# Sums of weights moved from GpSimd to VectorE, a new place for second-layer blocks, and one rectification in place of two

## The chip, the cores and the metric

The kernel runs on one core of a Trainium2 chip. The metric is the device time of one execution in microseconds. TensorE (PE in the profile) multiplies, VectorE (DVE), ScalarE (ACT) and GpSimd (POOL) work on elements, and SyncE (SP) issues the transfers. Each engine takes its instructions in order.

## The reference

Three stages follow each other; the change lies in the third, a mixture of four experts over all 2304 tokens.

```
attention through 32 memory slots     -> x: 2304 tokens x 512
x = relu(x @ w_in)**2 @ w_out         # 512 -> 2048 -> 512
p = domain_probs / sum(domain_probs)
for e in range(4):                    # moe2_w1: 512 -> 1024, moe2_w2: 1024 -> 512
    h = max(x @ w1[e], 0)
    out += p[:, e:e+1] * (h @ w2[e])
```

## The kernel before

Every float32 operand of a product is held as two parts, a high one and the low remainder. A product takes three matmuls for each piece of the contraction: high by high, high by low, low by high. The helper that makes the parts (`into`, lines 243 to 246, and `rectified`, lines 500 to 505) is a ScalarE instruction for the high part and a VectorE instruction for the low part.

The third stage goes over the 16 slabs `s` of 256 hidden units (four for each expert) twice. The first pass takes tokens 0 to 1023, the second tokens 1024 to 2047 and the last 256 tokens, called the rest.

**First pass.** The first layer of a slab is a 2 by 2 block product with seven products in place of eight, named b11, t1, b21, t2, t3, t4 and b22 in this order (`first_products`, line 507). Each product is two pieces of the contraction by three matmuls, six matmuls of 128x512. They add up in four PSUM banks u, m, v and t: u collects b11, then t2, then t3, and ScalarE copies it out (`copied`, line 526, copies `cc` or a copy that seeds another bank) after each, before the next product may add to it. v is seeded from u after b11, t from u after t3. `total` (line 561) completes one of four hidden blocks g11, g22, g21, g12: an addition on VectorE where a copy of u belongs to it (line 565), and then `rectified`. m holds t1 and b22; the addition for g22 reads m before b22 may add to it, and the addition for g12 empties m for the next slab.

The second layer of a slab is eight plain blocks (`second_l2`, line 476) of six matmuls each, for 128 tokens; the first four read g11 and g21, the last four g12 and g22. They use four PSUM banks in turn, and VectorE takes each into the accumulator (`taken`, line 493; ScalarE does it for the first slab). They are put into the list `todo` and issued during the first layer of the next slab, by `between` (line 820).

The weights of the pass come from the generator `weights` (line 253). For a slab it loads `ra`, the first layer's four blocks, splits two of them, forms four 128x256 sums (`combined`, line 301, into the tiles `s`) and splits these; then it does the same with `rb`, the second layer's. The sums are needed by the first layer's products (from `ra`) and, for the second pass, by its second layer (from `rb`). All parts are also written to DRAM for the second pass (`keep`). Four steps of the generator come after each slab in the source. The tiles `s` have one buffer each, `raw` has two, the first layer's weights have eight and the second layer's four.

**Second pass.** Both layers use seven products (`third_blocks`, line 586, `third_product`, line 624), in an order written out in `STEPS` and `LAST` (lines 619 and 620). The first slab's products run with the last eight blocks of the first pass between them (line 837). For the rest, `rest_l1` (line 667) multiplies the two halves f of a slab's hidden units, 12 matmuls of 128x256 each, into two banks of one PSUM tile, and rectifies each half by itself. `rest_l2` (line 680) of the slab before follows it. The PSUM tiles `two` have two buffers.

The order of the source is a priority, not the order on the engines: a planner at build time orders each engine's instructions by its own estimate of when their inputs are there, so a later instruction can be placed ahead of an earlier one.

Of the kernel before, what the change touches and what calls it, by code (L numbers as in the profile page):

```python
# [12 lines left out]
F32 = mybir.dt.float32  # L13
F32R = mybir.dt.float32r
AF = mybir.ActivationFunctionType
ALU = mybir.AluOpType
# [6 lines left out]
KT = DM // 128  # L23
# [5 lines left out]
NF2 = FS2 // 128  # L29
SE = F2 // FS2  # L30
S2 = E * SE
NB = 512
# [3 lines left out]
NR = NT - 4 * NB  # L36
# [3 lines left out]
def tile_kernel(  # L40
# [11 lines left out]
    nc = tc.nc  # L52
# [12 lines left out]
    def bank(tag):  # L65
        return (ps if tag in ("moe", "score") else ps_one).tile([128, 512], F32, tag=tag, name=tag, bufs=BANKS[tag])
# [234 lines left out]
    def combined(a11, a12, a21, a22, places):  # L301

        u = [p.tile([128, WC], F32, tag=tag, name=f"s{i}", bufs=1) for i, (p, tag) in enumerate(places)]
        t = [u[i // 2][:, (i % 2) * 256:(i % 2 + 1) * 256] for i in range(4)]
        nc.gpsimd.tensor_tensor(out=t[0], in0=a21, in1=a22, op=ALU.add)
        nc.gpsimd.tensor_tensor(out=t[1], in0=t[0], in1=a11, op=ALU.subtract)
        nc.gpsimd.tensor_tensor(out=t[2], in0=a11, in1=a21, op=ALU.subtract)
        nc.gpsimd.tensor_tensor(out=t[3], in0=a12, in1=t[1], op=ALU.subtract)
        return u

    kept = {}
# [150 lines left out]
    def rest():  # L462
        v = halves(8, KT, NR)
        for k in range(KT):
            put((v[:, 0, k], v[:, 1, k]), yacc[:, k, 4 * NB:])
        return v
# [33 lines left out]
    def rectified(c, n, g):  # L500
        nc.scalar.activation(g[:, 0, :n], c, AF.Relu)
        nc.vector.scalar_tensor_tensor(  # L502
            out=g[:, 1, :n], in0=c, scalar=0.0, in1=g[:, 0, :n].bitcast(F32), op0=ALU.max, op1=ALU.subtract
        )
        return g

    def first_products(w, x, total, seeded):

        def block(t, c):
            return [[w[t][:, h, c * 256 + k * 128:c * 256 + (k + 1) * 128] for k in range(2)] for h in range(2)]  # L510

        a = {"b11": (0, 0), "b21": (0, 1), "t1": (2, 0), "t4": (1, 1), "t2": (2, 1), "t3": (3, 0), "b22": (3, 1)}

        def product(po, name, first=True):
            wb, xb = block(*a[name]), x[name]
            i = 0
            for k in range(2):
                for lw, rx in ((0, 0), (0, 1), (1, 0)):
                    nc.tensor.matmul(  # L519
                        po, wb[lw][k], xb[:, rx, k], start=(first and i == 0), stop=(i == 5),  # L520
                        skip_group_check=not first,
                    )
                    i += 1

        def copied(p, seed=None):
            if seed is not None and seeded:
                nc.scalar.copy(seed, p)
                return None
            c = cp[0].tile([128, NB], F32, tag="c", name="cc")
            nc.scalar.copy(c, p)  # L530
            return c

        u, m, v, t = bank("moe"), bank("moe"), bank("moe"), bank("score")
        product(u, "b11")
        u1 = copied(u, v)
        yield
        product(m, "t1")
        yield
        product(v, "b21", first=not seeded)
        total("11", v, u1)  # L540
        yield
        product(u, "t2", first=False)
        u2 = copied(u)
        yield
        product(u, "t3", first=False)
        u3 = copied(u)
        total("22", m, u3)
        if seeded:
            copied(u, t)
        yield  # L550
        product(t, "t4", first=not seeded)
        total("21", t, None if seeded else u3)
        yield
        product(m, "b22", first=False)
        total("12", m, u2)
        yield

    def second_pair(s, x, between):
        g = {}

        def total(name, p, q):
            c = p
            if q is not None:
                c = cp[0].tile([128, NB], F32, tag="c", name="c")
                nc.vector.tensor_tensor(out=c, in0=p, in1=q, op=ALU.add)
            g[name] = rectified(c, NB, hp3[0].tile([128, 2, NB], F32R, tag="g", name="g"))

        for i, _ in enumerate(first_products(w_two[0, s], x, total, s > 0)):
            if i in (4, 5):
                between(i - 4)  # L570
        return [
            (lambda q=q: second_l2(s, q, (g["11"], g["21"]) if q < 4 else (g["12"], g["22"]), (q % 4) * 128))
            for q in range(8)
        ]
# [4 lines left out]
    def shares_of(e):  # L579
        nc.sync.dma_start(out=shares, in_=kept_p[e].partition_broadcast(128).rearrange("p (k n) -> p k n", k=KT))  # L580
# [83 lines left out]
            nc.vector.tensor_tensor(out=m[:, a], in0=po[:, a], in1=m[:, a], op=ALU.add)  # L664
            nc.sync.dma_start(out=outT[o:o + 128, j * NB:(j + 1) * NB], in_=m[:, a])

    def rest_l1(s, x, f, g, two):
        w = w_two[1, s]
        ph = two[:, f]
        i = 0  # L670
        for k in range(KT):
            for lw, rx in ((0, 0), (0, 1), (1, 0)):
                nc.tensor.matmul(  # L673
                    ph[:, :NR], w[f][:, lw, k * 128:(k + 1) * 128], x[:, rx, k],
                    start=(i == 0), stop=(i == 3 * KT - 1),
                )
                i += 1
        rectified(ph[:, :NR], NR, g[:, f])

    def rest_l2(s, g, ps_two):  # L680
        e = s // SE
# [43 lines left out]
    with tc.tile_pool(name="bdp", bufs=1) as bdp, tc.tile_pool(name="cv", bufs=1) as cv, \  # L725
# [6 lines left out]
        with tc.tile_pool(name="att", bufs=2) as att, tc.tile_pool(name="hp1", bufs=2) as hp, \  # L732
# [13 lines left out]
            for t in FIRST_LOADS.split():  # L746
                i = int(t[1])
# [8 lines left out]
            for t in PROGRAM.split():  # L756
                i = int(t[1]) if len(t) > 1 else 0
# [17 lines left out]
            out=p_sb, in0=p_sb, in1=p_sum.unsqueeze(2).to_broadcast([128, NT // 128, E]), op=ALU.mult  # L775
# [13 lines left out]
        with tc.tile_pool(name="ring", bufs=1) as rp, tc.tile_pool(name="tmp3", bufs=2) as tmp:  # L789
            ring = [rp.tile([128, KT, RING], F32R, name=f"ring{i}") for i in range(2)]  # L790
            for s in range(2, N1):
                last = s + 1 == N1
                for j in range(2 * B):
# [8 lines left out]
                    if last and j >= 4:  # L802
                        for _ in range(1 if j == 7 else 2):
                            x = next(steps)
            flush()
    with tc.tile_pool(name="cp2", bufs=6) as cp2, tc.tile_pool(name="w2p", bufs=4) as w2, \
            tc.tile_pool(name="hp3", bufs=6) as hp:
        cp.append(cp2)
        w2p.append(w2)
        hp3.append(hp)  # L810
        next(ws)
        next(ws)
        for e in range(E):
            nc.sync.dma_start(out=kept_p[e].rearrange("(t p) -> p t", p=128), in_=p_sb[:, 8:16, e])
        xr = rest()
        shares_of(0)
        later = []
        todo = []

        def between(i):  # L820
            for _ in range((len(todo) + 1) // 2 if i == 0 else len(todo)):
                todo.pop(0)()

        for s in range(S2):
            todo += second_pair(s, x, between)
            if s + 1 < S2:
                for _ in range(4):
                    next(ws)
        fetch(0)
        for x in prepare(1):  # L830
            pass

        def rest_tile():
            return hp.tile([128, 2, 2, NR], F32R, tag="g", name="gr")

        blocks, g = third_blocks(0, x, later)
        for i, _ in enumerate(blocks):
            if i in (4, 5):
                between(i - 4)
        singles.close()  # L840
        gr = rest_tile()
        later.pop(0)()
        with tc.tile_pool(name="ps_two", bufs=2, space=bass.MemoryType.PSUM) as ps_two:
            two = ps_two.tile([128, 2, NB], F32, tag="two", name="two")
            rest_l1(0, xr, 0, gr, two)
            rest_l1(0, xr, 1, gr, two)
            for s in range(1, S2):
                fetch(s)
                if s % SE == 0:
                    shares_of(s // SE)  # L850
                blocks, g_next = third_blocks(s, x, later)
                gr_next = rest_tile()
                for step in STEPS if s + 1 < S2 else LAST:
                    if step == "p":
                        next(blocks)
                    elif step == "t":
                        later.pop(0)()
                    elif step in A2:
                        third_product(s - 1, g, step, ps_two)
                    elif step[0] == "r":  # L860
                        two = ps_two.tile([128, 2, NB], F32, tag="two", name="two")
                        for f in range(NF2):
                            rest_l1(s, xr, f, gr_next, two)
                    elif step == "e":
                        rest_l2(s - 1, gr, ps_two)
                    else:
                        gather(step[:2], step[3:5], nc.gpsimd if step.endswith("*") else None)
                g, gr = g_next, gr_next
            rest_l2(S2 - 1, gr, ps_two)
            for i, j in ((0, 0), (1, 0), (0, 1), (1, 1)):  # L870
                third_plain(g, i, j, ps_two)
# [52 lines left out]
```

## Time and profile before

| | |
|---|---|
| median of three runs | 1144.48 us (1142.22 to 1147.76) |
| profiled execution | 1143.0 us, of which the span is 1141.2 us |
| busy, share of the span | TensorE 97%, VectorE 73%, ScalarE 52%, GpSimd 12% |
| granted TensorE clock, mean | 0.99 |
| first pass on TensorE | 399 us to 746 us of the span |

Times in the profile are microseconds from the start of the span. The busy share of TensorE counts matmuls that overlap in its pipeline, so it is no measure of lost time by itself; the distance between the starts of successive groups of matmuls is used for that. "Idle before" in square brackets is the time for which the engine did nothing before the instruction, with the instruction that released it.

### The profile page before, as it was taken

What the parts mean: (1) busy time and instruction counts of PE and PEld (TensorE: products, weight loads), DVE (VectorE), ACT (ScalarE), POOL (GpSimd) and SP (SyncE); (2) the same over time, 40 slices, a digit from 0 to 9 for tenths busy, and PEclk for the clock granted to TensorE, in tenths of its full rate; (3) what the DMA queues carried; (4) which work ended last, traced back from release to release, by engine and by line L of the source; (5) the groups of instructions that cost most, each with busy time, mean ns of one, the idle gap of its engine ahead of it and who ended that gap; (6) DMA issues with size and microseconds to landing.
All of it is one profiled execution on the core that took longest, in us unless ns stands there. A gap on an engine that the chain in (4) does not pass through costs nothing.

```text
span 1141.2 us, 16527 instructions
## 1 busy us (share of the span) xinstructions
PE 1101.7 (97%) x6142; PEld 934.8 (82%) x6142; DVE 827.4 (73%) x1366; ACT 589.0 (52%) x1178; POOL 132.3 (12%) x150
## 2 busy tenths in 40 slices
PE   5888999999999999999999999999999999999997
PEld 2667898999999977787888888888888888888886
DVE  6997989786446667768676776866766677776676
ACT  3776666565456464444444444355555555545541
POOL 0032000001000223333332431000000000000000
PEclk9798999999999999999999999999999999999999
DMA  9675222221020076767667577365545555554522
GB/s 330 223 196 57 75 75 74 75 74 38 1 93 1 38 308 244 304 232 308 244 260 268 228 278 272 133 204 181 198 155 165 168 185 176 181 196 148 163 95 93
DMA packets 63873, 192.23 MB, mean 168 GB/s; under 512 B 10801, under 2 KB 12849, under 8 KB 63793
## 3 DMA queue, kind: packets, MB, share of 16 engines
q1 hardware_dynamic: 63792, 191.18, 48.6%
q8 instruction: 48, 0.79, 0.3%
q14 instruction: 33, 0.26, 0.1%
HBM read 119.31 MB, written 71.84 MB: 168 GB/s over the span
## 4 chain that ended last, share of the span: by engine, by line
PE 53%; DVE 2%; DMA 1%; issue 0%; ACT 0%; POOL 0%; SPq 0%; DVEq 0%; POOLq 0%
PE moe L519 18%; PE two L637 12%; PE fold L485 5%; PE two L673 4%; PE two L688 4%; PE score L519 3%; PE turn L485 3%; PE memory L485 3%; PE two L660 1%; DMA rb<-in_wts 1%; DVE acc L498 0%; DVE c L602 0%; DVE w L245 0%; DMA kept<-w 0%; DVE acc L644 0%
## 5 line engine op out<-in xcount | busy, mean ns | idle before, releaser
L519 PE MATMUL moe<-mem,f 128*128 128x512 f32 x576 | 146.7, 389 | 0.0
L519 PEld LDWEIGHTS moe<-mem,f 128*128 128x128 f32 x576 | 107.9, 188 | 22.9 <-ACT mem L411 0.2
L644 DVE TENSOR_TENSOR acc<-two,acc 128x1024 f32<-128x1024 f32 x56 | 68.5, 1224 | 63.9 <-PE two L637 62.6
L519 PE MATMUL moe<-mem,ws 128*128 128x512 f32 x384 | 99.1, 393 | 6.5 <-ACT cc L530 5.4
L485 PE MATMUL fold<-w,g 128*128 128x512 f32 x384 | 100.9, 389 | 0.0
L519 PEld LDWEIGHTS moe<-mem,ws 128*128 128x128 f32 x384 | 70.7, 188 | 24.9 <-ACT cc L530 9.2
L637 PE MATMUL two<-gt,f 128*128 128x512 f32 x360 | 88.9, 389 | 0.0
L485 PEld LDWEIGHTS fold<-w,g 128*128 128x128 f32 x384 | 72.1, 188 | 15.1
L372 PE MATMUL moe<-mem 128*128 128x288 f32 x432 | 75.4, 309 | 6.0 <-ACT mem L202 4.4
L393 PE MATMUL moe<-ring,wo 128*128 128x384 f32 x432 | 80.9, 335 | 0.0
L637 PEld LDWEIGHTS two<-gt,f 128*128 128x128 f32 x360 | 67.6, 188 | 14.0
L372 PEld LDWEIGHTS moe<-mem 128*128 128x128 f32 x432 | 63.5, 194 | 18.2 <-issue 8.1
L642 ACT COPY acc<-two 128x1024 f32<-128x1024 f32 x49 | 49.7, 1014 | 49.6 <-PE two L637 49.6
L393 PEld LDWEIGHTS moe<-ring,wo 128*128 128x128 f32 x432 | 75.1, 188 | 0.0
L381 DVE TENSOR_TENSOR ring<-g,ring 128x288 fp32r<-128x288 f32 x96 | 45.0, 472 | 31.4 <-ACT ring L380 31.2
L530 ACT COPY cc<-moe 128x512 f32<-128x512 f32 x65 | 38.1, 586 | 52.0 <-PE moe L519 52.0
L379 ACT ACTIVATE g<-r 128x288 f32<-128x288 f32 x128 | 57.1, 446 | 1.9 <-DVE ring L381 0.3
L498 DVE SCALAR_TENSOR_TENSOR acc<-fold,p_sb,acc 128x512 f32<-128x512 f32 x60 | 44.7, 745 | 14.5 <-PE fold L485 14.2
L673 PEld LDWEIGHTS two<-mem,f 128*128 128x128 f32 x384 | 49.1, 191 | 7.0 <-DVE gr L502 4.9
L673 PE MATMUL two<-mem,f 128*128 128x256 f32 x384 | 51.8, 284 | 1.9 <-DVE gr L502 1.5
L647 POOL TENSOR_TENSOR acc<-acc 128x1024 f32<-128x1024 f32 x1 | 2.4, 2396 | 417.4 <-DVE acc L644 417.4
L485 PE MATMUL turn<-w,g 128*128 128x512 f32 x192 | 50.7, 391 | 0.0
(184 smaller groups left out, 2403.9 us busy)
## 6 DMA issues: line engine op xcount, KB each, us to landing
f<-kept SPq DMA_DIRECT2D x128, 512.0 KB, 4.5
kept<-w SPq DMA_DIRECT2D x64, 512.0 KB, 3.2
kept<-ws SPq DMA_DIRECT2D x32, 512.0 KB, 3.6
kept<-mem SPq DMA_DIRECT2D x32, 512.0 KB, 2.7
raw<-in_wts SPq DMA_DIRECT2D x28, 512.0 KB, 3.3
ra<-in_wts SPq DMA_DIRECT2D x16, 512.0 KB, 6.5
rb<-in_wts SPq DMA_DIRECT2D x16, 512.0 KB, 5.2
kv<-in_kv SPq DMA_DIRECT2D x24, 256.0 KB, 4.5
```

Source lines behind the costliest of these rows:

```text
L372: nc.tensor.matmul(ph[:, :HS], folded[b][:, lw + hg, fc], atts[b][:, rx + hg, cs], start=(i == 0), stop=(i == 5))
L379: nc.scalar.activation(g, r, AF.Square)
L381: nc.vector.tensor_tensor(out=gl[:, f], in0=g, in1=gh[:, f].bitcast(F32), op=ALU.subtract)
L393: nc.tensor.matmul(po[:, :n], w[:, lw], rg[:, f], start=(i == 0), stop=(i == 3 * nf - 1))
L485: nc.tensor.matmul(po, g[f][:, lg, at:at + 128], w[:, rw], start=(i == 0), stop=(i == 3 * NF2 - 1))
L498: nc.vector.scalar_tensor_tensor(out=oa, in0=po, scalar=pe, in1=oa, op0=ALU.mult, op1=ALU.add)
L519: nc.tensor.matmul(po, wb[lw][k], xb[:, rx, k], start=(first and i == 0), stop=(i == 5), skip_group_check=not first,)
L637: nc.tensor.matmul(po[:, a], w[:, lw, o + a * 128:o + (a + 1) * 128], g[xb][:, rx], start=(i == 0 and not seeded), stop=(i == 2), skip_gro ...
L642: nc.scalar.copy(m, po)
L644: nc.vector.tensor_tensor(out=m, in0=po, in1=m, op=ALU.add)
L673: nc.tensor.matmul(ph[:, :NR], w[f][:, lw, k * 128:(k + 1) * 128], x[:, rx, k], start=(i == 0), stop=(i == 3 * KT - 1),)
L688: nc.tensor.matmul(po[:, a], g[:, f, lg, a * 128:(a + 1) * 128], w[:, rw], start=(i == 0), stop=(i == 3 * NF2 - 1))
```

## The change

It has three parts. The sums in `combined` go from GpSimd to VectorE. The second-layer blocks of the slab before, four after t3 and four after t4 until now, come two after b11, three after t2 and three after t3; the copy of u that seeds t goes ahead of the copy for g22's addition. And `rest_l1` takes its own PSUM tile, multiplies both halves and rectifies them with one ScalarE and one VectorE instruction of 128 x 512.

```
 def combined(a11, a12, a21, a22, places):
-        nc.gpsimd.tensor_tensor(out=t[0], in0=a21, in1=a22, op=ALU.add)
-        nc.gpsimd.tensor_tensor(out=t[1], in0=t[0], in1=a11, op=ALU.subtract)
-        nc.gpsimd.tensor_tensor(out=t[2], in0=a11, in1=a21, op=ALU.subtract)
-        nc.gpsimd.tensor_tensor(out=t[3], in0=a12, in1=t[1], op=ALU.subtract)
+        nc.vector.tensor_tensor(out=t[0], in0=a21, in1=a22, op=ALU.add)
+        nc.vector.tensor_tensor(out=t[1], in0=t[0], in1=a11, op=ALU.subtract)
+        nc.vector.tensor_tensor(out=t[2], in0=a11, in1=a21, op=ALU.subtract)
+        nc.vector.tensor_tensor(out=t[3], in0=a12, in1=t[1], op=ALU.subtract)
...
         product(u, "t3", first=False)
+        if seeded:
+            copied(u, t)
         u3 = copied(u)
         total("22", m, u3)
-        if seeded:
-            copied(u, t)
...
         for i, _ in enumerate(first_products(w_two[0, s], x, total, s > 0)):
-            if i in (4, 5):
-                between(i - 4)
+            between(i)
...
-    def rest_l1(s, x, f, g, two):
+    def rest_l1(s, x, g, ps_two):
         w = w_two[1, s]
-        ph = two[:, f]
-        i = 0
-        for k in range(KT):
-            for lw, rx in ((0, 0), (0, 1), (1, 0)):
-                nc.tensor.matmul(
-                    ph[:, :NR], w[f][:, lw, k * 128:(k + 1) * 128], x[:, rx, k],
-                    start=(i == 0), stop=(i == 3 * KT - 1),
-                )
-                i += 1
-        rectified(ph[:, :NR], NR, g[:, f])
+        two = ps_two.tile([128, 2, NB], F32, tag="two", name="two")
+        for f in range(NF2):
+            i = 0
+            for k in range(KT):
+                for lw, rx in ((0, 0), (0, 1), (1, 0)):
+                    nc.tensor.matmul(
+                        two[:, f, :NR], w[f][:, lw, k * 128:(k + 1) * 128], x[:, rx, k],
+                        start=(i == 0), stop=(i == 3 * KT - 1),
+                    )
+                    i += 1
+        c = two[:, :, :NR]
+        nc.scalar.activation(g[:, :, 0], c, AF.Relu)
+        nc.vector.scalar_tensor_tensor(
+            out=g[:, :, 1], in0=c, scalar=0.0, in1=g[:, :, 0].bitcast(F32), op0=ALU.max, op1=ALU.subtract
+        )
...
         def between(i):
-            for _ in range((len(todo) + 1) // 2 if i == 0 else len(todo)):
-                todo.pop(0)()
+            for _ in range({0: 2, 3: 3, 4: 3}.get(i, 0)):
+                if todo:
+                    todo.pop(0)()
```

The first slab of the second pass calls `between(i)` in the same way, and the callers of `rest_l1` pass the pool in place of a tile.

## Rows read from the trace of the kernel before

**Rows 1.** Page, engines: busy us, share of the span, instructions.
```profile
PE 1101.7 (97%) x6142; PEld 934.8 (82%) x6142; DVE 827.4 (73%) x1366; ACT 589.0 (52%) x1178; POOL 132.3 (12%) x150
```
**Rows 2.** Waits of TensorE, 399 to 746 us: total us, times, longest.
```profile
PE moe L519 <- ACT cc L530: 5.4, 3, 2.4
...
PE moe L519 <- DVE c L565: 1.1, 1, 1.1
```
**Rows 3.** Timeline of TensorE, an early slab: start us, us, instructions, idle before.
```profile
434.04 1.52 PE L519 MATMUL moe<-mem,w 128*128 128x512 f32 x6
435.40 1.52 PE L519 MATMUL moe<-mem,ws 128*128 128x512 f32 x6
436.76 1.29 PE L485 MATMUL fold<-w,g 128*128 128x512 f32 x5
440.50 1.66 PE L519 MATMUL moe<-mem,ws 128*128 128x512 f32 x6 [2.44 <-ACT cc L530]
442.00 1.52 PE L485 MATMUL turn<-w,g 128*128 128x512 f32 x6
```
**Rows 4.** Timeline of ScalarE, the same stretch.
```profile
436.80 0.62 ACT L244 CAST mem<-s 128x512 fp32r<-128x512 f32 x1 [0.52 <-POOL s L308]
...
439.35 0.62 ACT L244 CAST ws<-s 128x512 fp32r<-128x512 f32 x1 [0.41 <-POOL s L306]
439.87 0.58 ACT L530 COPY cc<-moe 128x512 f32<-128x512 f32 x1
```
**Rows 5.** Instructions on the tiles s: ns min/median/max, first and last start.
```profile
L245 DVE TENSOR_TENSOR ws<-s,ws x30: 673/680/1228, 402.0 to 684.3; 128x512 fp32r<-128x512 f32 x30
...
L308 POOL TENSOR_TENSOR s<-ra,s x15: 728/1180/1294, 387.2 to 678.3; 128x256 f32<-128x256 f32 x15
```
**Rows 6.** Timeline of TensorE, a settled slab: b22, t4, the next block, b22.
```profile
599.64 1.52 PE L519 MATMUL moe<-mem,ws 128*128 128x512 f32 x6
...
613.34 1.52 PE L519 MATMUL score<-mem,w 128*128 128x512 f32 x6
614.70 1.52 PE L485 MATMUL fold<-w,g 128*128 128x512 f32 x6
...
620.14 1.52 PE L519 MATMUL moe<-mem,ws 128*128 128x512 f32 x6
```
**Rows 7.** Windows, a settled slab: length, busy us and instructions of each engine.
```profile
600.00:620.50 20.50, 20.50 (x92) 16.82 (x91) 14.88 (x23) 9.07 (x17) 6.50 (x8) 1.00 0.65 257
```
**Rows 8.** Groups by line and form, VectorE: busy us, mean ns, idle before.
```profile
L502 DVE SCALAR_TENSOR_TENSOR gr<-two,gr 128x256 fp32r<-128x256 f32 x32 | 13.4, 420 | 1.3 <-ACT gr L501 0.5
L502 DVE SCALAR_TENSOR_TENSOR g<-moe,g 128x512 fp32r<-128x512 f32 x15 | 10.3, 689 | 27.4 <-ACT g L501 27.4
```
**Rows 9.** Timeline of VectorE, the settled slab: the rectification of t4's product.
```profile
615.53 0.69 DVE L502 SCALAR_TENSOR_TENSOR g<-score,g 128x512 fp32r<-128x512 f32 x1
```
**Rows 10.** Instructions on the tile rb, 590 to 645 us: issue to landing.
```profile
DMA to landing us min/median/max: 5.2/5.2/5.2
```
**Rows 11.** Timeline of TensorE, a settled slab of the second pass.
```profile
793.49 1.33 PE L688 MATMUL two<-f,gr 128*128 128x512 f32 x5
794.65 1.63 PE L673 MATMUL two<-mem,f 128*128 128x256 f32 x12
```
**Rows 12.** Timeline of TensorE and of VectorE, the last slab.
```profile
1116.73 2.91 PE L688 MATMUL two<-f,gr 128*128 128x512 f32 x12
1121.15 1.70 PE L673 MATMUL two<-mem,f 128*128 128x256 f32 x12 [1.51 <-DVE gr L502]
1122.69 3.12 PE L688 MATMUL two<-f,gr 128*128 128x512 f32 x12
...
1120.68 0.41 DVE L502 SCALAR_TENSOR_TENSOR gr<-two,gr 128x256 fp32r<-128x256 f32 x1
...
1126.07 1.40 DVE L498 SCALAR_TENSOR_TENSOR acc<-two,p_sb,acc 128x512 f32<-128x512 f32 x2
```

More of the change, by code (lines that the diff above doesn't have):

```diff
@@ L837, in tile_kernel @@
         for i, _ in enumerate(blocks):
-            if i in (4, 5):
-                between(i - 4)
+            between(i)
         singles.close()
@@ L843, in tile_kernel @@
         with tc.tile_pool(name="ps_two", bufs=2, space=bass.MemoryType.PSUM) as ps_two:
-            two = ps_two.tile([128, 2, NB], F32, tag="two", name="two")
-            rest_l1(0, xr, 0, gr, two)
-            rest_l1(0, xr, 1, gr, two)
+            rest_l1(0, xr, gr, ps_two)
             for s in range(1, S2):
@@ L860, in tile_kernel @@
                     elif step[0] == "r":
-                        two = ps_two.tile([128, 2, NB], F32, tag="two", name="two")
-                        for f in range(NF2):
-                            rest_l1(s, xr, f, gr_next, two)
+                        rest_l1(s, xr, gr_next, ps_two)
                     elif step == "e":
```

## The prediction

> **What bounds the kernel now.** I read the page's engine table first: TensorE is busy for 97% of the span and VectorE for 73% [rows 1]. What TensorE has to multiply is the same after the change, so the change can only win what TensorE loses between matmuls. Next I read the TensorE timeline for a price of one block of six 128x512 matmuls: starts 1.36 us apart (434.04 to 435.40, and 435.40 to 436.76) [rows 3]. A settled slab of the first pass holds seven first-layer products and eight second-layer blocks, fifteen blocks or 20.40 us, and the same product (b22) comes back after 20.50 us (599.64 to 620.14) [rows 6]. So a settled slab has 0.1 us to give, no more. Then I read the list of waits, for TensorE alone and inside the first pass. TensorE itself stood still four times there: three times for a ScalarE copy of a product's bank (5.4 us), once for a VectorE addition (1.1 us) [rows 2]. The reader is to see that this is a matter of four places among sixteen slabs, not of the slab as such.
>
> One of the four in full [rows 3]: t2 (435.40) ends its issue at 436.76, five matmuls of a second-layer block follow, 1.13 us at 0.227 each, to 437.89, and t3 starts only at 440.50. That is 2.61 us lost, and t3 itself then takes 1.50 us (to 442.00) instead of 1.36, so 2.75 where the list of waits has 2.44: 0.31 more. With that the four cost 6.5 + 4 x 0.31 = 7.7 us.
>
> Why t3 was late is on ScalarE's timeline [rows 4]. t3 adds into the bank u and must wait for the copy `cc` of u as t2 left it. The copy runs at 439.87, three microseconds after t2. ScalarE's queue is in order, and ahead of the copy stand casts of the weights' sums `s`, which wait for GpSimd (0.52 and 0.41 us on the record). GpSimd's sums take 1.18 us in the median for the slowest of the four, and VectorE's splits, 0.68 us in the median, go up to 1.23 while the two engines work at once [rows 5].
>
> **The change, part by part.**
>
> *Sums on VectorE.* It takes eight GpSimd instructions of 128x256 from each slab and gives VectorE eight. No VectorE row shows these; the nearest is the 128x256 rectification, 0.420 us from a PSUM source [rows 8], and I take that: 8 x 0.42 = 3.4 us per slab. Lower bound half the 128x512 duration, 0.34 us each, upper bound one stretched as the splits are, 1.23 us for 512, or 0.61. VectorE is busy 14.88 us of 20.5 in a settled slab [rows 7], so it goes to 18.2 (17.6 to 19.8), and TensorE hides all of it as long as no consumer is late. On the path: 0. The four sums in a row take 1.7 us instead of up to 4 x 1.18 = 4.7 [rows 5], so the casts behind which the copy stood come up to 3 us earlier. What waits now: the sum's first operand is a fresh transfer, which lands 5.2 us after its issue [rows 10]. GpSimd could wait for it at no cost; on VectorE every eviction queued behind it waits too. That is a rival below.
>
> *Second-layer blocks spread 2, 3, 3.* Nothing is added. In the source, four blocks stood after t3 and four after t4; the planner had pulled part of the first one ahead of t3 as a filler. Now two stand after b11, three after t2, three after t3. The gap after t2 is covered by 3 x 1.36 = 4.08 us of work: in the slab above t3 would come up at 436.76 + 4.08 = 440.84, later than the 440.50 at which its copy was ready even with all of today's lateness. The gap before t1, where the addition was late once, is covered by b11 and two blocks, also 4.08 us, where the wait's whole length was 1.1 [rows 2]. So both edits by themselves remove these waits: -7.7 us. Bounds: -7.7, and -4.9 if one stop of 2.75 comes back. What has less cover afterwards: b22 waits for the addition that empties m, and t3 to b22 has three blocks and t4 (5.4 us) in place of eight blocks and t4. Its chain is two ScalarE copies and one VectorE addition, each under 0.7 us by the 128x512 rows [rows 8]; it fits. The swapped order of the two copies delays the one for the addition by one copy, which this cover holds too. The settled slab's 0.1 us of seams I leave as it is (0, bounds -1.5 and +1.5 for sixteen slabs).
>
> *Last tokens' two blocks rectified as one.* Two ScalarE and two VectorE instructions become one each: 2 x 0.420 against 0.69 for 512 columns [rows 8], 0.15 us of VectorE per slab, hidden. The gain is in order: today the second half of these products waits for the VectorE rectification of the first half, and the planner fills in. In a settled slab of the second pass it puts five matmuls of the other product between (793.49 to 794.65, 1.16 us against 5 x 0.227 = 1.13) [rows 11], a seam of 0.03 us; two fewer of these in each of 15 slabs is about 0.9 us. I take -0.5 (0 to -0.9). In the last slab there is nothing to fill in with: 2.72 us after 1116.73 TensorE is free, and the second half starts at 1121.15, with a recorded wait of 1.51 for that rectification: 1.7 us lost [rows 12]. Merged, both halves run on, and the last block (today 1122.69) waits for the merged rectification instead: in VectorE's queue at 1120.68 with 0.69 us it ends at 1121.4, so it could start 1.3 us earlier. But VectorE works there without a pause to 1127.4 (1126.07 plus 1.40) [rows 12], and the final blocks need the PSUM buffer that these last instructions free. I take -0.9 (0 to -1.7). The Trainium skill (Perfetto Trace Analysis, Optimizing Scalar/DVE Operations) has a rule against this edit: where the two engines are not saturated but make others wait, breaking instructions up lets work finish sooner. By that rule the term would be zero or a small loss, and the sum 0.9 us higher; the row on the 1.51 us wait speaks for the merge, since here it is the split that makes TensorE wait.
>
> **The sum**, against the profiled execution's own time, 1143.0 us (span 1141.2): -7.7 - 0.5 - 0.9 = -9.1, so 1133.9. The median of the runs shown is 1144.48, 1.5 above the profiled one; I forecast a median, so 1133.9 + 1.5 = 1135.4.
>
> **Rivals.**
>
> *A. The stops are only halved* (chance 0.20). The planner places each instruction by its own estimate of when its input is there; the profile shows it was wrong by 3 us for the copy in three slabs. If it places the casts ahead of the copy again and the sums are now late in VectorE's queue behind evictions, the wait for the copy shrinks but stays. For it: the casts stand ahead of the copy [rows 4]. Against: 4.08 us of cover. Half of 7.7 gone: -3.9 - 1.4 = -5.3, or 1139.2.
>
> *B. No effect* (chance 0.13). The order on TensorE is not that of the source: the planner already moves part of a block ahead of t3 [rows 3]. If it lays out the new source so that the fillers are again used up before the gaps, the four stops stay, moved: 1144 (1142 to 1146).
>
> *C. Slower: VectorE becomes late* (chance 0.17). The sums wait on VectorE for the transfer, and behind them stands the rectification of t4's product, which the first second-layer block of the next slab needs. Today that is ready 1.5 us after t4 has been issued (614.70 to 615.53 + 0.69) [rows 6, 9], and the consumer comes four blocks and five products later. Afterwards only b22 and b11 lie between, 2.72 us, and the low part is needed 1.13 us further on, at the sixth matmul: 3.85 - 1.5 = 2.3 us is the point from which it decides. A sum queued right after its transfer's issue would hold VectorE for up to 5.2 us [rows 10], 2.9 over. For it: VectorE at 18.2 of 20.5. Against: 2.3 us are free in each slab and the transfer is issued half a slab ahead. At 1 us for each of 15 slabs: +15 - 1.4 + the stops gone -7.7, or about 1150. The Trainium skill (the same section) says that a saturated VectorE may give work to GpSimd, the opposite of this edit; 14.88 of 20.5 us is not saturated, 18.2 is near it, and which it is decides between this rival and the forecast.
>
> **How the numbers follow.** Forecast 0.50, A 0.20, B 0.13, C 0.17. I take a 0.5% change, 5.7 us, as about what a measurement of this kernel tells from none: the line is at 1138.8. The forecast lies below it nearly always (0.47 of 0.50), A in four of ten cases (0.08): 0.55 faster. Same takes the rest of A (0.12), the rest of the forecast (0.03), B (0.12) and a small C (0.02): 0.29. Slower: 0.16. The low end is the sum with every bound at its best (-7.7 - 1.5 - 0.9 - 1.7 = -11.8, or 1132.7) with 0.7 for the scatter of a median; the high end takes in A and B and the mildest of C.
>
> **What would show it.** Right: TensorE's waits for `cc` and for the addition to m gone from the list for the first pass; the slabs of 399 to 526 us 20.5 us long each; VectorE near 18 us in a settled slab with GpSimd at 0; the start of the second pass 7 to 8 us earlier. Wrong on the sums: VectorE idle before the sums' lines for the transfer `rb` or `ra`, and TensorE waiting for the rectified `g` or for an eviction. Wrong on the merge: TensorE waiting in the last slab for the merged rectification for over 1 us, or for PSUM buffers of the final blocks.

## The result, and the profile after

The changed kernel took 1128.89 us in the median (1127.51 to 1131.16) against 1143.35 us for the kernel before in the same sessions: a ratio of 0.987, with an interval of 0.983 to 0.991. A second set of runs gave 1128.74 against 1142.78 us, ratio 0.990 (0.987 to 0.993). So it is faster, by 14 us where 9.1 were forecast, and the time lies below the low end of the range, 1132.0.

The distances between starts on TensorE's timeline divide the profiled executions into four parts. The first pass runs from its first product to the first matmul for the last tokens.

| us | before | after | difference | forecast |
|---|---|---|---|---|
| ahead of the first pass | 399.20 | 396.06 | -3.1 | 0 |
| first pass | 346.51 | 336.53 | -10.0 | -7.7 |
| from there to the last matmul | 390.59 | 388.25 | -2.3 | -1.4 |
| after the last matmul | 4.9 | 4.9 | 0 | 0 |

The mark between the first pass and what follows does not stand at the same matmul in both kernels: from the first product to the mark there are 1486 matmuls before and 1482 after. Before, the planner had drawn four of the six matmuls of a second-pass product ahead of the mark, 0.9 us of work, and two come behind it (TensorE, before):

```profile
745.71 1.60 PE L673 MATMUL two<-mem,f 128*128 128x256 f32 x12
747.14 0.63 PE L519 MATMUL moe<-mem,f 128*128 128x512 f32 x2
```

In the changed kernel all six come behind it:

```profile
732.59 3.04 PE L673 MATMUL two<-mem,f 128*128 128x256 f32 x24
735.46 1.55 PE L519 MATMUL moe<-mem,f 128*128 128x512 f32 x6
```

At equal work the first pass gave 9.1 us (9.98 less 0.91) and the part behind it 3.2.

The page's engine row of the changed kernel, to be read beside [rows 1]: GpSimd is all but empty, VectorE went from 73% to 76%, TensorE's 97% says nothing of 15 us.

```profile
PE 1096.3 (97%) x6142; PEld 936.2 (83%) x6142; DVE 854.0 (76%) x1478; ACT 585.8 (52%) x1162; POOL 20.9 (2%) x22
```

TensorE's timeline in the same early slab as [rows 3] (start, length, instructions): t2, three second-layer blocks, t3, the next block. All starts are 1.36 us apart; in the list of TensorE's waits there is none left in the first pass, where [rows 2] had four.

```profile
433.00 1.52 PE L519 MATMUL moe<-mem,ws 128*128 128x512 f32 x6
434.36 1.52 PE L485 MATMUL fold<-w,g 128*128 128x512 f32 x6
435.72 1.52 PE L485 MATMUL memory<-w,g 128*128 128x512 f32 x6
437.08 1.52 PE L485 MATMUL fold<-w,g 128*128 128x512 f32 x6
438.44 1.52 PE L519 MATMUL moe<-mem,ws 128*128 128x512 f32 x6
439.80 1.52 PE L485 MATMUL turn<-w,g 128*128 128x512 f32 x6
```

ScalarE in the same stretch, beside [rows 4]: the copy `cc` is no longer behind the casts of the sums. It starts 0.2 us after t2 has been issued, and the casts that wait (now for VectorE) come behind it and hold nobody.

```profile
433.20 0.60 ACT L501 ACTIVATE g<-moe 128x512 fp32r<-128x512 f32 x1 [0.80 <-PE moe L519]
434.56 0.59 ACT L530 COPY cc<-moe 128x512 f32<-128x512 f32 x1 [0.76 <-PE moe L519]
437.11 1.14 ACT L244 CAST ws<-s 128x512 fp32r<-128x512 f32 x2 [1.96 <-DVE s L306]
```

A settled slab as a window (length, busy time and instructions of each engine), beside [rows 7]: 32 records on VectorE where there were 23, and 2.0 us more busy time, not the 3.4 of the forecast. The sums' records last 0.42 us, as assumed, but follow each other at 0.33 to 0.34 us.

```profile
598.00:618.40 20.40, 20.40 (x91) 16.89 (x90) 16.92 (x32) 9.27 (x17) 0.00 (x0) 1.00 0.67 258
```

The last slab on TensorE, beside [rows 12]: both halves for the last tokens run on as 24 matmuls, and 1.5 us of waiting became 0.25 and 0.30.

```profile
1100.70 3.04 PE L673 MATMUL two<-mem,f 128*128 128x256 f32 x24
1103.58 2.91 PE L692 MATMUL two<-f,gr 128*128 128x512 f32 x12
1106.74 3.02 PE L692 MATMUL two<-f,gr 128*128 128x512 f32 x12 [0.25 <-DVE gr L680]
1109.60 2.88 PE L659 MATMUL two<-mem,f 128*128 128x512 f32 x12
1112.78 3.02 PE L659 MATMUL two<-mem,f 128*128 128x512 f32 x12 [0.30 <-DVE acc L498]
```

### The profile page after: what moved, and what is told of

Same layout as the page of the kernel before. It is cut to its first block, busy times and chain, and to the rows that moved or that the text cites. A ratio compares the mean times of both kernels' runs of the same rounds, so it can differ in the third digit from the quotient of the medians.

```text
span 1125.7 us, 16428 instructions
## 1 busy us (share of the span) xinstructions
PE 1096.3 (97%) x6142; PEld 936.2 (83%) x6142; DVE 854.0 (76%) x1478; ACT 585.8 (52%) x1162; POOL 20.9 (2%) x22
## 4 chain that ended last, share of the span: by engine, by line
PE 90%; DVE 6%; ACT 1%; DMA 1%; issue 0%; SPq 0%; POOL 0%; DVEq 0%; ACTq 0%; POOLq 0%
PE moe L519 23%; PE two L636 12%; PE moe L393 9%; PE fold L485 8%; PE moe L372 5%; PE turn L485 4%; PE memory L485 4%; PE two L673 4%; PE score L519 4%; PE two L692 3%; PE turn L393 3%; PE score L393 2%; PE memory L393 2%; PE fold L344 2%; PE memory L372 2%; PE score L372 1%
## 5 line engine op out<-in xcount | busy, mean ns | idle before, releaser
L485 PE MATMUL fold<-w,g 128*128 128x512 f32 x384 | 97.6, 389 | 0.0
L519 PE MATMUL moe<-mem,w 128*128 128x512 f32 x192 | 48.9, 389 | 0.0
L485 PE MATMUL memory<-w,g 128*128 128x512 f32 x192 | 48.7, 389 | 0.0
```

The source lines that it names most:

```text
L485: nc.tensor.matmul(po, g[f][:, lg, at:at + 128], w[:, rw], start=(i == 0), stop=(i == 3 * NF2 - 1))
L519: nc.tensor.matmul(po, wb[lw][k], xb[:, rx, k], start=(first and i == 0), stop=(i == 5), skip_group_check=not first,)
```

## The experiments

All kernels have the same instructions for 260 us, so they are compared by two lengths that start behind that: the first pass, and the time from its first product to the last matmul (737.1 us before).

| us | first pass | to the last matmul | start of the first pass |
|---|---|---|---|
| before | 346.5 | 737.1 | 399.2 |
| sums alone | 339.4 | 729.9 | 395.8 |
| spread alone (with the swapped copies) | 339.0 | 728.6 | 399.1 |
| merge alone | 347.5 | 736.1 | 399.5 |
| all three, first and second profile | 336.5, 336.5 | 724.8, 724.8 | 396.1, 399.8 |
| all but the sums | 339.6 | 727.7 | 400.0 |
| all but the spread | 339.4 | 727.9 | 400.4 |
| all but the merge | 336.6 | 726.3 | 395.5 |
| all but the swapped copies | 336.6 | 726.2 | 396.4 |
| blocks placed 0, 4, 4 | 337.4 | 724.6 | 400.2 |
| sums done twice | 336.6 | 724.6 | 396.9 |
| sums done three times | 358.5 | 746.8 | 397.0 |
| one late addition on GpSimd | 336.6 | 728.1 | 398.3 |

The first pass of the kernel before, of the sums alone, the merge alone, all but the spread, and of the blocks placed 0, 4, 4 holds four matmuls, 0.9 us, more than that of the others (the mark, as above). The second length holds the same work in all.

**One edit at a time.** Sums alone:

```
-        nc.gpsimd.tensor_tensor(out=t[0], in0=a21, in1=a22, op=ALU.add)
+        nc.vector.tensor_tensor(out=t[0], in0=a21, in1=a22, op=ALU.add)
...
```

> Only the sums go to VectorE; blocks and rectification as before. Theory 1 (the spread cures the first pass, the sums only shorten lateness): the gap before t3 keeps its 1.1 us of cover, so stops shrink but stay; the first pass on TensorE (346.5 us before, 336.5 with all three edits) is 340 to 343 us, a settled slab stays at 20.50. Theory 2 (GpSimd's slow sums alone make the copies late): all four stops of 7.7 us go, first pass at 339 or less, with settled slabs still at 20.50. On the start: if the 3.1 us by which the first pass began earlier in the changed kernel is chance, its start lies anywhere from 395 to 400 us; if the sums cause it, it lies at 396.

Ratio 0.994 (0.992 to 0.996). First pass 339.4 us, between the two theories (340 to 343, and 339 or less). TensorE has no listed wait in it: the four stops are gone, as theory 2 had it. The seams stay: slabs of 20.50, and three early ones of 20.6 to 20.7. A place like that of [rows 3] on TensorE's timeline: four matmuls of a block, 0.91 us from 431.68, and t3 at 432.76, only 0.17 us late.

```profile
431.68 1.07 PE L485 MATMUL fold<-w,g 128*128 128x512 f32 x4
432.76 1.65 PE L519 MATMUL moe<-mem,ws 128*128 128x512 f32 x6
434.25 0.39 PE L485 MATMUL fold<-w,g 128*128 128x512 f32 x1
```

Spread alone:

```
-            if i in (4, 5):
-                between(i - 4)
+            between(i)
...
+            for _ in range({0: 2, 3: 3, 4: 3}.get(i, 0)):
```

> Only the blocks are spread 2, 3, 3, with the two copies of u swapped; sums on GpSimd, two rectifications. Theory 1: 4.08 us of cover hold all of today's lateness: no stop of TensorE in the first pass, slabs of 20.40, first pass 336.5 to 338 us. Theory 2: ScalarE still waits for GpSimd's 4.7 us of sums and the copies come late by more than the cover in the early slabs: first pass over 340 us.

Ratio 0.992 (0.989 to 0.995). First pass 339.0 us, between the two theories. Settled slabs are 20.40, but four early ones are 21.34, 20.48, 21.50 and 20.72, 2.4 us over in all. The first of them on ScalarE and TensorE: ScalarE still waits 1.13 and 1.66 us for GpSimd, `cc` comes at 441.64, over four microseconds after t2 was issued (437.38), and the cover of 4.08 us falls 0.8 us short.

```profile
438.35 0.62 ACT L244 CAST ws<-s 128x512 fp32r<-128x512 f32 x1 [1.13 <-POOL s L306]
440.63 0.62 ACT L244 CAST ws<-s 128x512 fp32r<-128x512 f32 x1 [1.66 <-POOL s L308]
441.15 0.59 ACT L501 ACTIVATE g<-moe 128x512 fp32r<-128x512 f32 x1
441.64 0.58 ACT L530 COPY cc<-moe 128x512 f32<-128x512 f32 x1
```

TensorE there:

```profile
440.11 1.52 PE L485 MATMUL fold<-w,g 128*128 128x512 f32 x6
442.27 1.65 PE L519 MATMUL moe<-mem,ws 128*128 128x512 f32 x6 [0.65 <-ACT cc L530]
```

So neither theory holds by itself. At equal work the sums alone take 7.1 us from the first pass and the spread alone 6.6, they share 4.7 of it, and only both together leave no slab above 20.4.

Merge alone:

```
-        rectified(ph[:, :NR], NR, g[:, f])
...
+        nc.scalar.activation(g[:, :, 0], c, AF.Relu)
```

> Only the last tokens' two rectifications become one. Theory 1: it gives all that the second pass gained: a slab of 24.71 instead of 24.81 us, the last slab about 1.5 us shorter, 2.3 us in all, 0.2% of the time; first pass unchanged at 346.5 us with its four stops. Theory 2: the second pass gained because its inputs from the first came earlier or GpSimd is quiet: slabs stay at 24.81 and only the wait in the last slab goes, 1 to 1.5 us.

Ratio 1.000 (0.998 to 1.002); the timing can't tell it from no change. The trace can: 388.6 us from the first matmul for the last tokens to the last matmul instead of 390.6, slabs of 24.75 instead of 24.81, not the 24.71 that theory 1 had. So something else had a share in the second pass. The first pass is 1.0 us longer, so 1.1 us are left: its third slab has 3.9 us over 20.40 where it had 2.7. Why an edit of the second pass lengthens a stop of the first is not shown.

The changed kernel once more, without an edit:

> The changed kernel once more. Theory 1: first pass 336.5 us, second pass to the last matmul 388.2 us, as in its first profile; what lies ahead of the first pass differs between executions of the same instructions, so its start is anywhere from 395 to 400 us. Rival: the start is 396 us again and 399 in kernels without the sums on VectorE. The time is 1131 us if the 3.1 us ahead of the first pass were chance, 1128.5 if they belong to the change.

The time was 1128.7 us. Both lengths are the same as in its first profile to 0.05 us, but the start lies at 399.84 instead of 396.06. It is one program, so these 3.8 us are no effect of the change.

**One edit taken back.** The sums back on GpSimd:

```
-        nc.vector.tensor_tensor(out=t[0], in0=a21, in1=a22, op=ALU.add)
+        nc.gpsimd.tensor_tensor(out=t[0], in0=a21, in1=a22, op=ALU.add)
...
```

> The changed kernel with the sums back on GpSimd. From the start of the first pass to the last matmul: 737.1 us before, 724.8 with all three, 728.6 with the spread alone. Theory (the parts add where they don't cure the same stop): 727 to 728 us, the first pass about 339, with stops of some 2.6 us in all in the early slabs, one of them for a rectified g. Rival (the merge needs VectorE's sums): 728.6 or more.

As expected: 727.7 us, with 1.5 us of listed waits on TensorE in the first pass, 0.6 of them for a rectified `g`. The blocks and the copies back in their places:

```
-            between(i)
+            if i in (4, 5):
+                between(i - 4)
...
```

> The changed kernel with the blocks and the copies of u as before. Theory: first pass 339.4 us as with the sums alone, settled slabs 20.50; with the merge 728 to 729 us to the last matmul, second-pass slabs 24.75. Rival: the first pass is near 337 since sums and merge together are enough.

First pass 339.4, slabs 20.50 and 24.75, 727.9 in all: 0.1 below the expected range. Two rectifications again:

```
-        nc.scalar.activation(g[:, :, 0], c, AF.Relu)
...
+        rectified(ph[:, :NR], NR, g[:, f])
```

> The changed kernel with two rectifications for the last tokens' blocks. Theory: first pass 336.5 us, second-pass slabs 24.77 as with the spread alone, the wait for the first rectification back in the last slab: 725.5 to 726.5 us to the last matmul. Rival (the copies' new order did it all): 724.8.

As expected, 726.3 us, and the wait in the last slab is back, on TensorE:

```profile
1102.26 2.91 PE L687 MATMUL two<-f,gr 128*128 128x512 f32 x12
1106.59 1.70 PE L672 MATMUL two<-mem,f 128*128 128x256 f32 x12 [1.42 <-DVE gr L502]
```

The two copies of u in their old order:

```
-        if seeded:
-            copied(u, t)
         u3 = copied(u)
         total("22", m, u3)
+        if seeded:
+            copied(u, t)
```

> The changed kernel with the two copies of u back in their old order (the copy for g22's addition ahead of the one that seeds t). Theory: the swap is what shortened the seam ahead of t4's product in both passes, which the merge alone did not (24.75 us per slab of the second pass with the merge alone, 24.71 with all, 24.77 with the spread and the swap alone): a second-pass slab is 24.75 us here; the first pass has five blocks' time between t3 and t4, so its slabs stay at 20.40. Rival: the swap does nothing, 24.71.

Second-pass slabs of 24.77 us, and 1.4 us in all: the swap counts, in the second pass alone. There t4's product comes 2.0 us after t3 has been issued and waits for the copy that seeds t. TensorE without the swap has 1.47 us from that product to the next:

```profile
774.84 1.63 PE L519 MATMUL score<-mem,f 128*128 128x512 f32 x6
776.31 1.98 PE L636 MATMUL two<-gt,f 128*128 128x512 f32 x8
```

With it, in the changed kernel, 1.40 us:

```profile
773.98 1.57 PE L519 MATMUL score<-mem,f 128*128 128x512 f32 x6
775.38 1.98 PE L636 MATMUL two<-gt,f 128*128 128x512 f32 x8
```

**How many blocks where.**

```
-            for _ in range({0: 2, 3: 3, 4: 3}.get(i, 0)):
+            for _ in range({3: 4, 4: 4}.get(i, 0)):
```

> The changed kernel with the eight blocks placed 0, 4, 4: none after b11, four after t2, four after t3. Theory 1 (what stopped TensorE ahead of t1 was the late addition on m, and two blocks after b11 cover it): one or more stops of about 1 us for that addition come back, first pass 337.5 to 340 us against 336.5. Theory 2 (with the sums on VectorE the addition is in time anyway): no stop, 336.5 to 337.

No stop, slabs of 20.40, theory 2. The first pass is 0.9 us longer, which is the four matmuls of the mark and no stop; in all it is 0.2 us less. With the sums on VectorE the two blocks after b11 aren't needed; what matters is that whole blocks stand between t2 and t3.

**How much room VectorE has.** Each sum twice or three times over, the same values written again:

```
+        for _ in range(2):
             nc.vector.tensor_tensor(out=t[0], in0=a21, in1=a22, op=ALU.add)
...
```

> The changed kernel with each of the eight sums on VectorE done twice over (the second writes the same values). It asks how much room VectorE has: it was busy 16.9 us of a 20.40 us slab. Eight more at about 0.34 us from start to start are 2.7 us, 19.6 us. Theory 1 (VectorE hides all as long as a slab's sum fits): slabs stay at 20.40 to 20.6, first pass under 340 us. Theory 2 (the queue is in order, so lateness shows before it is full): slabs of 20.8 to 21.5 with TensorE waiting for rectified g or for evictions, first pass 343 to 355 us.

> The same with each sum done three times: about 22.3 us of VectorE work against 20.40. Both theories: VectorE is the bound, slabs of 21.8 to 23 us, first pass 358 to 375 us, TensorE waiting for rectified g and for evictions in every slab. The step from two to three times gives the price of a sum where VectorE is the bound: 8 sums at 0.34 to 0.42 us, 2.7 to 3.4 us per slab if it was full at two, less where it was not.

Twice: no slab is longer, 724.6 us, with VectorE busy 19.6 us of 20.40 on average in two early slabs (windows).

```profile
500.00:520.40 20.40, 20.40 (x92) 16.90 (x91) 19.80 (x40) 9.02 (x16) 0.00 (x0) 1.00 0.71 274
520.40:540.80 20.40, 20.40 (x92) 16.90 (x91) 19.35 (x39) 8.97 (x16) 0.00 (x0) 1.00 0.66 244
```

Theory 1, to within 1 us of full. Three times: VectorE is busy without a pause (window of nearly two slabs) and slabs are 21.7 us, a tenth of a microsecond below the range I had; the first pass is at the low end of its range.

```profile
600.00:640.00 40.00, 38.12 (x166) 30.52 (x165) 40.00 (x88) 16.96 (x29) 0.00 (x0) 1.00 0.68 244
```

TensorE's waits in the first pass (total us, times, longest): most for the casts of the sums, not for `g` as both theories had it.

```profile
PE moe L520 <- ACT ws L244: 9.0, 10, 1.0
PE fold L486 <- DVE acc L499: 3.5, 1, 3.5
```

**An attempt on what is left.** In the last slab VectorE works without a pause and TensorE waits twice; one of five additions was given to GpSimd:

```
-    LAST = "... m4 p r e m6+m1 m7+m6 m4+m7 ..."
+    LAST = "... m4 p r e m6+m1* m7+m6 m4+m7 ..."
```

> The changed kernel, and in the last slab one of the five additions of 128x1024 that VectorE does in a row goes to GpSimd (m6+m1). Theory (VectorE without a pause is what limits the end, two stops of 0.4 us on TensorE): these stops go, 0.5 to 0.9 us from the last slab, 723.9 to 724.3 us to the last matmul. Rival: GpSimd needs 2.4 us where VectorE needs 1.2, and the next addition waits for it: no gain or 0.5 us lost.

It lost 3.3 us, far more than the rival had. The addition on GpSimd:

```profile
1101.73 2.45 POOL L646 TENSOR_TENSOR acc<-acc 128x1024 f32<-128x1024 f32 x1 [0.36 <-ACT acc L641]
```

A VectorE instruction that started 0.1 us after it:

```profile
1101.84 2.88 DVE L245 TENSOR_TENSOR mem<-c,mem 128x512 fp32r<-128x512 f32 x1
```

The low part of g took 2.88 us instead of 0.68 and ended 0.5 us after the addition. All that stood behind it on VectorE came later by as much, and TensorE waited 2.26 us for the merged rectification. No version here beats the changed kernel by more than 0.2 us, so none was timed against it.

## Why the prediction was wrong where it was

**Direction and mechanism held.** All four stops went, the copy comes right behind t2, VectorE hides the sums, TensorE waits nowhere in the first pass. The merge took away most of the wait in the last slab.

**First pass: -7.7 forecast, -10.0 by the mark, -9.1 at equal work. The term that failed is "the settled slab's 0.1 us of seams I leave as it is (0, bounds -1.5 and +1.5 for sixteen slabs)".** The slabs went from 20.50 to 20.40, which is fifteen blocks of 1.36 without a rest. In eleven slabs without a stop that is 1.1 us; the four with stops had 7.9 us over 20.40, where I had 7.7. Together that is all of the 9.1. The seam can be read on the timeline of the kernel before, at t3 of the settled slab of [rows 6]: 1.44 us to the next start instead of 1.36. The list of waits has the weight loads of such products waiting 9.4 us for `cc`, 17 times, those at the three long stops among them; after the change it is one wait of 0.2 us.

```profile
608.02 1.60 PE L519 MATMUL moe<-mem,ws 128*128 128x512 f32 x6
609.46 1.32 PE L485 MATMUL turn<-w,g 128*128 128x512 f32 x5
```

I had used this 0.1 us to say that a settled slab had no more to give, and then did not count it eleven times.

**"Both edits by themselves remove these waits" held nearly for the sums and not for the spread.** The sums alone leave no listed wait, and 0.5 us above 20.50 in four early slabs. For the spread I took the lateness of one slab (3.1 us) and set it against 4.08 us. With the spread alone the planner orders ScalarE's queue anew, the waits for GpSimd grow, and the copy came over four microseconds late. Rival A described this: casts ahead of the copy, stops shrunk but not gone. It is what the two kernels with the spread and without the sums on VectorE do. With all three edits there is nothing of it.

**Second pass: -1.4 forecast, -2.3 by the mark, -3.2 at equal work, beyond the best of its bounds (-0.9 and -1.7, -2.6 together). The step that failed is the swap of the two copies.** I priced it only as a delay for g22's addition in the first pass, and did not see that the same function serves the second pass, where t4's product waits for the copy that now goes first. Undone, it costs 1.4 us. The merge, the only part that I had priced there, was nearer: 2.0 us alone, 1.5 when it is taken back. In the slabs the seam was sized at 0.03 us for two places; they went from 24.81 to 24.71, with the merge alone to 24.75. In the last slab I took -0.9. From its last first-layer product to the last matmul it went from 23.0 to 21.5 us, which is more, but with one of the two taken back it is 22.3 (the merge) or 22.2 (the swap): half of it is the swap's. The buffer that I feared for held TensorE for 0.3 us.

**The Trainium skill's rule** that breaking instructions up may let work be completed sooner (Perfetto Trace Analysis, Optimizing Scalar/DVE Operations) did not hold here: split again, the kernel lost 1.5 us to the last matmul, since TensorE's second half waited for the first half's rectification.

**Rival C did not come in the first pass.** VectorE waited 0.5 us once for a transfer ahead of a sum, not up to 5.2 us. I had the room too small: 18.2 us was a sum of record lengths that overlap; measured 16.9, and twice the sums still fit. The point from which it decides lies between 16 and 24 sums in a slab.

**Ahead of the first pass the sums cost 0.6 us, where I had 0.** The first four run at 265 to 269 us, in the stage before, and the low part of the fold, which TensorE's next matmuls wait for, comes 0.7 us later behind them on VectorE. The changed kernel, TensorE (window 265 to 270):

```profile
267.73 1.69 PE L344 MATMUL fold<-wf,vt 64*32 64x512 f32 x16 [0.51 <-DVE mem L351]
```

From the 1801st matmul (at 245 to 250 us) to the first pass it is 150.7 us in all ten profiles with the sums on VectorE and 150.1 in all four without.

**The rest is the start of the execution.** With the right terms the sum is -9.1 - 3.2 + 0.6 = -11.7 us. Put in place of -9.1 it makes the forecast 1132.8, inside the range. The median came 3.9 us lower still, and no run shows a cause of that in the change: 1.7 of it is the median of the kernel before, 1142.78 in sixteen runs where the three that I had gave 1144.48. The start of the first pass lay between 395.5 and 400.4 us in the thirteen profiles made after the forecast, and at 396.1 and 399.8 for one and the same program; by the 801st matmul, at 108.5 to 113.6 us, up to which all kernels have the same instructions, the profiles are already as far apart. All four kernels with GpSimd's sums start late (399.1 or more), three of the ten others too; that the change shifts how often a start is late is not ruled out.

## What to carry to other kernels

Where the bound engine's period is known (blocks times the price of one), count what each period lacks to it times the number of periods, even if it is 0.1 us: it goes when the order gets better. Look up every caller of a function whose order is changed; a swap made for one pass can gain in another. Count the matmuls between two marks before comparing the times between them. And a fix that gives slack and one that takes lateness away are worth timing apart: here each cured most of the same stops, and the sum of both alone was half again what they gave together.

## What the runs showed of the hardware

A GpSimd addition of 2.45 us held a VectorE instruction with two operands in SBUF for nearly all its length: 2.88 us against 0.68. The Trainium skill says that such an instruction contends with a GpSimd instruction that reads SBUF, over a port pair that works as an exclusive lock (SBUF — State Buffer, Who interferes with whom), and this trace agrees. The changed kernel has one such place of its own in the last slab: beside an older GpSimd addition of 2.40 us (1096.72) a VectorE instruction that started at 1097.75 took 1.92 us instead of 0.68. In the kernel before, the lock works both ways. A split that began 0.01 us after a sum took 1.28 us, the sum 0.74; another began 0.02 us ahead of a sum and took 0.69, the sum 1.27 (GpSimd's two sums):

```profile
437.44 0.74 POOL L305 TENSOR_TENSOR s<-ra 128x256 f32<-128x256 f32 x1 [0.68 <-POOL s L308]
417.73 1.27 POOL L305 TENSOR_TENSOR s<-ra 128x256 f32<-128x256 f32 x1 [0.70 <-POOL s L308]
```

The fifteen sums of that trace beside which VectorE did nothing took 0.73 to 0.75 us, the 33 that began during a split 1.05 to 1.28. So the 1.18 us that the prediction read from [rows 5] as the price of a sum is 0.74 and a wait for VectorE.

Between 83 and 113 us, while the attention stage still runs, executions of the same instructions drift apart by some 3 us. ScalarE stands still ahead of single copies and casts there, not at the same one each time. The changed kernel's second profile, ScalarE, has 2.38 us between two casts:

```profile
88.06 0.37 ACT L350 CAST mem<-fold 128x256 fp32r<-128x256 f32 x1 [0.67 <-PE fold L344]
90.81 0.37 ACT L350 CAST mem<-fold 128x256 fp32r<-128x256 f32 x1 [2.38 <-PE moe L393]
```

In its first profile the same two follow each other at once:

```profile
87.20 0.65 ACT L350 CAST mem<-fold 128x256 fp32r<-128x256 f32 x2 [0.67 <-PE fold L344]
```

In six of the seven profiles with a late start, and in one of the seven with an early one, a stop of over 1.1 us a little later ends by a releaser outside of what the profile shows ("remote"). What ScalarE waited for was not tried and stays open.
